# Retention attention and a SoLU layer on one core: chunks paired on halves of the partitions, 64x64 products, u centred

## Chip, cores and metric

One core of one Trainium2 chip. The time is device time in microseconds, from the first to the last instruction of a launch and what lies around them; the median of three runs of the kernel before is 229.86 us (229.05 to 230.84).

## The reference

```python
# q, k, v: [8 batches, 8 heads, 576 tokens, 64]
scores = scale * np.matmul(q, k.transpose(0, 1, 3, 2))        # scale = 1/8
gamma = 1.0 - 2.0 ** (-5.0 - np.arange(H))
Dmat = np.where(rel >= 0, gamma[:, None, None] ** rel, 0.0)   # rel = query - key
x = np.matmul(scores * Dmat, v)          # tokens of all heads side by side: [4608, 512]
h = x @ w_in                             # [4608, 1024]
e = np.exp(h - max(h)); sm = e / (sum(e) + 1e-9)
solu = h * sm
ln = (solu - mean(solu)) / np.sqrt(var(solu) + 1e-6) * g_ln
out = ln @ w_out                         # [4608, 512]
```

The decay is a product of a power for the query, one for the key and a mask, so the attention can run chunk by chunk: within a chunk with scores, across chunks with a state per head (64x64) that is scaled by gamma^128 from chunk to chunk.

## The kernel before

The 4608 tokens are 36 chunks of 128 tokens: four whole chunks of each batch, two batches in turn, and a ninth chunk that holds the last 64 tokens of both. For each chunk n the steps are:

- `lq`, `lk`, `lv`: load 128 tokens x 8 heads x 64 in f32 through the queue of SP (line 150). `q`, `k`, `v`: cast to f16, with the decay powers on q and v (lines 171 to 175, mostly on GpSimd, POOL).
- `tp`: eight transposes of q and k on TensorE (line 200); `qkT`: their copy out of PSUM (line 208).
- `sc`: scores, keys x queries, eight matmuls on a half of the rows each (line 221); `m0`, `m1`: the mask, on VectorE (DVE), 512 columns each (line 229).
- `kp`: the chunk's own contribution to the state, k times v (line 249); `t`: added to the state before (294, 296); `s16`, `s32`: the scaled state, in f16 with zeros beside each head's block, and in f32 (303, 313).
- `xs` (state times q, line 268) and `xv` (masked scores times v, line 282) make x transposed in PSUM; `xT` copies it out.
- `mm1`: h, 8 matmuls of 512 columns (342). `max`, `exp`, `solu` (359, 374, 410): u = h * exp(h - max), with its sum; `nmu`: minus its mean (420); `sq`: the sum of (u - mean)^2 on ScalarE (ACT, 438); `w1`, `w2`, `pow`: the row's scale `rs` (401, 446, 452).
- `lp`: eight transposes of u (460), `uT`: copy out, `mm2`: 8 matmuls of 512 columns (476), `osb`: scaled by `rs` (488, 492), `st`: store (502).

The mean of u is not taken off u: the columns of `w_out` are centred once at the start instead. `ws` scales `w_out` by `g_ln`, `mean` multiplies it by a tile of ones (549), and `cw` subtracts (560).

The order of all steps is written out: `FIRST`, then `LOOP` for chunks 12 to 29, then `LAST`. Every engine, and the queue of SP, takes its instructions in that order. PSUM has four banks in turn for all small products and two pairs of banks for h. `warm` issues matmuls on zeros early on.

Of the kernel before, what the change touches and what calls it, by code (L numbers as in the profile page):

```python
# [17 lines left out]
def _np_tables():  # L18


    g = 1.0 - 2.0 ** (-5.0 - np.arange(H, dtype=np.float64))
    p = np.arange(P)
    gq = (g[None, :] ** p[:, None]) / 8.0
    gk = g[None, :] ** (-p[:, None])
    gqt = (g[None, :] ** (p % 64)[:, None]) / 8.0
    gkt = g[None, :] ** (-(p % 64)[:, None])


    gs = np.zeros((P, 4))
    gd = np.zeros((P, 4, 2))  # L30
    for e in range(2):
        for hp in range(4):
            gs[e * 64 : e * 64 + 64, hp] = g[2 * hp + e] ** 128.0
        gd[e * 64 : e * 64 + 64, :, e] = gs[e * 64 : e * 64 + 64]
    small = np.concatenate([gq, gk, gqt, gkt, gs, gd.reshape(P, 8)], axis=1).astype(np.float32)
    return small
# [3 lines left out]
def kernel(  # L40
# [19 lines left out]
    small_np = _np_tables()  # L60

    const = ctx.enter_context(tc.tile_pool(name="const", bufs=1))
    load = ctx.enter_context(tc.tile_pool(name="load", bufs=8))
    qh = ctx.enter_context(tc.tile_pool(name="qh", bufs=4))
    kvh = ctx.enter_context(tc.tile_pool(name="kvh", bufs=6))
    att = ctx.enter_context(tc.tile_pool(name="att", bufs=3))
    stp = ctx.enter_context(tc.tile_pool(name="stp", bufs=2))
    moe = ctx.enter_context(tc.tile_pool(name="moe", bufs=3))
    two = ctx.enter_context(tc.tile_pool(name="two", bufs=2))
    dead = ctx.enter_context(tc.tile_pool(name="dead", bufs=1))  # L70
    utp = ctx.enter_context(tc.tile_pool(name="utp", bufs=5))
    tiny = ctx.enter_context(tc.tile_pool(name="tiny", bufs=6))
    ps = ctx.enter_context(tc.tile_pool(name="ps", bufs=1, space=bass.MemoryType.PSUM))
    ps_h = ctx.enter_context(tc.tile_pool(name="ps_h", bufs=1, space=bass.MemoryType.PSUM))


    chunks = []
    for g in range(B // 2):
        for c in range(4):
            chunks += [((2 * g,), c), ((2 * g + 1,), c)]  # L80
        chunks.append(((2 * g, 2 * g + 1), 4))
    NCH = len(chunks)

    def rows(n):
        bs, c = chunks[n]
        if c < 4:
            return [(slice(0, P), bs[0], c * P)]
        return [(slice(64 * i, 64 * i + 64), b, 4 * P) for i, b in enumerate(bs)]

    small = const.tile([P, 44], FP, name="small")  # L90
    tris = const.tile([P, 2, P], FP, name="tris")
    ident = const.tile([P, P], F16, name="ident")
    ones = const.tile([P, P], F16, name="ones")
    zeros = const.tile([P, 512], F16, name="zeros")
    mhalf = const.tile([P, 1], FP, name="mhalf")
    gln = const.tile([P, NF], FP, name="gln")
    g32 = const.tile([P, NF], FP, name="g32")
    w_in32 = const.tile([P, 4, DFF], FP, name="w_in32")
    w_out32 = const.tile([P, NF, DM], FP, name="w_out32")
    w_in16 = const.tile([P, 4, DFF], F16, name="w_in16")  # L100
    w_raw16 = const.tile([P, NF, DM], F16, name="w_raw16")
    w_out16 = const.tile([P, NF, DM], F16, name="w_out16")
    mean_sb = const.tile([P, DM], FP, name="mean_sb")
    gq, gk = small[:, 0:8], small[:, 8:16]
    gqt, gkt = small[:, 16:24], small[:, 24:32]
    gs = small[:, 32:36]
    gd = small[:, 36:44].rearrange("p (a b) -> p a b", a=4)

    T = {}

# [9 lines left out]
    def new(key, make):  # L120

        if key not in T:
            T[key] = make()
        return T[key]


    turn = {"bank": 0, "h": 0}

    def bank(shape, dtype, name):
        turn["bank"] += 1  # L130
        return ps.tile(shape, dtype, tag=f"bank{turn['bank'] % 4}", name=name)

    def h_banks(name):
        turn["h"] += 1
        return ps_h.tile([P, DFF], FP, tag=f"h{turn['h'] % 2}", name=name)


# [6 lines left out]


    def load_rows(name, src, n):
        t = load.tile([P, H, D], FP, name=name)
        for pp, b, s0 in rows(n):
            m = pp.stop - pp.start
            nc.sync.dma_start(  # L150
                out=t[pp], in_=src[b, :, s0 : s0 + m, :].rearrange("h p d -> p h d")
            )
        T[name, n] = t

    @step
    def lq(n, j, eng):
        load_rows("qf", q, n)

    @step
    def lk(n, j, eng):  # L160
        load_rows("kf", k, n)

    @step
    def lv(n, j, eng):
        load_rows("vf", v, n)

    def cast(name, to, pool, n, eng, table):
        src = T.get((name, n))
        t = pool.tile([P, H, D], F16, name=to)
        if table is None:  # L170
            copy(eng, t, src)
        else:
            vec(eng).tensor_tensor(  # L173
                out=t, in0=src, in1=table.unsqueeze(2).to_broadcast([P, H, D]), op=ALU.mult
            )
        T[to, n] = t

    def is_tail(n):
        return chunks[n][1] == 4

    @step
    def q_(n, j, eng):
        cast("qf", "q16", qh, n, eng or "g", gqt if is_tail(n) else gq)

    @step
    def k_(n, j, eng):
        cast("kf", "k16", kvh, n, eng or "g", None)

    @step
    def v_(n, j, eng):  # L190
        cast("vf", "v16", kvh, n, eng or "g", gkt if is_tail(n) else gk)


    @step
    def tp(n, j, eng):
        t = bank([P, 2, 4, P], F16, "tp")
        for i, src in enumerate((T.get(("q16", n)), T["k16", n])):
            s2 = src.rearrange("p h d -> p (h d)")
            for hp in range(4):
                nc.tensor.transpose(  # L200
                    out=t[:, i, hp], in_=s2[:, hp * P : (hp + 1) * P], identity=ident
                )
        T["tp", n] = t

    @step
    def qkT(n, j, eng):
        t = att.tile([P, 2, 4, P], F16, name="qkT")
        copy(
            eng or "v", t.rearrange("p a b c -> p (a b c)"),
            T.get(("tp", n)).rearrange("p a b c -> p (a b c)"),  # L210
        )
        T["qkT", n] = t

    @step
    def sc(n, j, eng):
        t = T["qkT", n]
        s = [bank([P, 4, P], FP, f"sc{e}") for e in range(2)]
        for hp in range(4):
            for e in range(2):
                dd = slice(64 * e, 64 * e + 64)  # L220
                nc.tensor.matmul(  # L221
                    out=s[e][:, hp], lhsT=t[dd, 1, hp], rhs=t[dd, 0, hp], start=True, stop=True,
                )
        T["sc", n, 0], T["sc", n, 1] = s

    def mask(n, e):
        i = 1 if is_tail(n) else 0
        r = att.tile([P, 4, P], F16, name=f"ret{e}")
        nc.vector.tensor_tensor(  # L229
            out=r, in0=T.get(("sc", n, e)), in1=tris[:, i : i + 1].to_broadcast([P, 4, P]),  # L230
            op=ALU.mult,
        )
        T["ret", n, e] = r

    @step
    def m0(n, j, eng):
        mask(n, 0)

    @step
    def m1(n, j, eng):  # L240
        mask(n, 1)

    @step
    def kp(n, j, eng):
        t = bank([P, 4, D], FP, "kp")
        k16, v16 = T.get(("k16", n)), T["v16", n]
        for hp in range(4):
            for e in range(2):
                nc.tensor.matmul(  # L249
                    out=t[64 * e : 64 * e + 64, hp], lhsT=k16[:, 2 * hp + e],  # L250
                    rhs=v16[:, 2 * hp + e], start=True, stop=True,
                )
        T["kp", n] = t


    def x_tile(n):
        first = ("x", n) not in T
        return first, new(("x", n), lambda: bank([P, 4, P], FP, "x"))

    @step  # L260
    def xs(n, j, eng):
        bs, c = chunks[n]
        first, x = x_tile(n)
        t = T["qkT", n]
        w = P // len(bs)
        for hp in range(4):
            for i, b in enumerate(bs):
                nc.tensor.matmul(  # L268
                    out=x[:, hp, i * w : (i + 1) * w],
                    lhsT=T["s16", b, c][:, hp].rearrange("p e d -> p (e d)"),  # L270
                    rhs=t[:, 0, hp, i * w : (i + 1) * w],
                    start=first, stop=True, skip_group_check=True,
                )
                first = False

    @step
    def xv(n, j, eng):
        first, x = x_tile(n)
        v16 = T["v16", n]
        for hp in range(4):  # L280
            for e in range(2):
# [420 lines left out]
```

## Time and profile before

| | |
|---|---|
| median of three runs | 229.86 us |
| span of the profiled execution, first to last instruction (its own time beside it is not listed) | 228.4 us |
| busy: PE, DVE, ACT, POOL | 216.1, 190.8, 167.1, 169.4 us |
| mean granted TensorE clock | 0.991 |
| moved by DMA | 42.34 MB in 120795 packets, 114496 of them under 512 B |

All figures of the trace come from one execution. PE is TensorE's matmuls, PEld its weight loads, SPq what the queue of SP issues. Lnnn is a line of the kernel that the profile belongs to. In the timeline a row is: start, length, engine, line, operation, tiles, how many were merged. A matmul's length has its way through the array in it, so the pace of a row of matmuls is read from the starts. Groups have: busy time, mean length in ns, and the idle time before them with what ended it.

### The profile page before, as it was taken

What the parts mean: (1) busy time and instruction counts of PE and PEld (TensorE: products, weight loads), DVE (VectorE), ACT (ScalarE), POOL (GpSimd) and SP (SyncE); (2) the same over time, 40 slices, a digit from 0 to 9 for tenths busy, and PEclk for the clock granted to TensorE, in tenths of its full rate; (3) what the DMA queues carried; (4) which work ended last, traced back from release to release, by engine and by line L of the source; (5) the groups of instructions that cost most, each with busy time, mean ns of one, the idle gap of its engine ahead of it and who ended that gap; (6) DMA issues with size and microseconds to landing.
All of it is one profiled execution on the core that took longest, in us unless ns stands there. A gap on an engine that the chain in (4) does not pass through costs nothing.

```text
span 228.4 us, 5672 instructions
## 1 busy us (share of the span) xinstructions
PE 216.1 (95%) x2181; PEld 122.1 (53%) x2181; DVE 190.8 (84%) x346; ACT 167.1 (73%) x270; POOL 169.4 (74%) x244
## 2 busy tenths in 40 slices
PE   7879689899999999999999999999999999999991
PEld 2334255555655655556555555555665565555461
DVE  1229999999997995899989999999889999898740
ACT  2075459877879799777778777777898777849970
POOL 2234999789969969799858998999958998655320
PEclk9999889999999999999999999999999999999999
DMA  6999999999999599999999887898955064111125
GB/s 159 250 353 312 231 228 206 212 197 191 244 225 239 110 236 236 254 221 265 216 264 218 188 198 156 204 226 180 211 144 138 3 176 103 47 49 47 46 74 159
DMA packets 120795, 42.34 MB, mean 185 GB/s; under 512 B 114496, under 2 KB 114752, under 8 KB 120768
## 3 DMA queue, kind: packets, MB, share of 16 engines
q1 hardware_dynamic: 119728, 41.98, 80.9%
q8 instruction: 17, 0.28, 0.6%
q10 hardware_dynamic: 1040, 0.00, 0.2%
q14 instruction: 10, 0.08, 0.1%
HBM read 32.53 MB, written 9.44 MB: 184 GB/s over the span
## 4 chain that ended last, share of the span: by engine, by line
PE 81%; DVE 8%; SPq 4%; DMA 3%; issue 1%; ACT 1%; DVEq 0%; ACTq 0%
PE o L476 27%; PE h L342 26%; PE lp L460 7%; PE tp L200 6%; PE sc L221 4%; PE x L282 4%; DMA vf<-in_v_dram 3%; PE x L268 3%; PE kp L249 3%; SPq L150 2%; DVE w_out L560 2%; DVE nm L359 1%; SPq L522 1%; DVE ret L229 1%; PE hh L332 1%
## 5 line engine op out<-in xcount | busy, mean ns | idle before, releaser
L342 PE MATMUL h<-w_in,xT 128*128 128x512 f16 x280 | 67.8, 387 | 1.6 <-DVE xT L118 1.5
L476 PE MATMUL o<-w_out,uT 128*128 128x512 f16 (+1 forms) x296 | 67.6, 373 | 0.0
L303 POOL TENSOR_TENSOR s<-t,small 128x512 f16<-128x512 f32 x32 | 33.5, 1048 | 19.7 <-DVE t L296 10.7
L229 DVE TENSOR_TENSOR ret<-sc,tris 128x512 f16<-128x512 f32 x72 | 46.4, 679 | 1.1 <-PE sc L221 1.0
L410 DVE SCALAR_TENSOR_TENSOR u<-h,e 128x1024 f16<-128x1024 f32 x35 | 42.6, 1217 | 2.6 <-ACT e L374 2.6
L173 POOL TENSOR_TENSOR q<-qf,small 128x512 f16<-128x512 f32 x35 | 36.9, 1055 | 9.8 <-DMA qf<-in_q_dram 9.8
L359 DVE TENSOR_REDUCE nm<-h 128x1 f32<-128x1024 f32 x35 | 42.5, 1214 | 1.4 <-PE h L342 1.3
L374 ACT ACTIVATE e<-h,nm 128x1024 f32<-128x1024 f32 x35 | 38.9, 1111 | 6.4 <-DVE nm L359 6.3
L438 ACT ACTIVATE sq<-u,nmu 128x1024 f16<-128x1024 f16 (+1 forms) x37 | 41.7, 1129 | 0.1
L476 PEld LDWEIGHTS <-uT 128*128 128x128 f16 x296 | 27.3, 98 | 26.9
L342 PEld LDWEIGHTS <-xT 128*128 128x128 f16 x280 | 26.1, 99 | 28.9 <-issue 2.3
L116 ACT CAST xT<-x 128x512 f16<-128x512 f32 x34 | 19.9, 584 | 25.8 <-PE x L268 19.3
L173 POOL TENSOR_TENSOR v<-vf,small 128x512 f16<-128x512 f32 x34 | 35.8, 1055 | 0.0
L116 ACT COPY uT<-lp 128x1024 f16<-128x1024 f16 x33 | 33.3, 1013 | 2.5 <-PE lp L460 2.5
L452 POOL TENSOR_TENSOR rs<-w,mhalf 128x1 f32<-128x1 f32 x36 | 20.1, 560 | 13.8 <-DVE w L446 11.9
L492 ACT ACTIVATE o_sb<-o,rs 128x512 f32<-128x512 f32 (+1 forms) x36 | 24.5, 681 | 5.7 <-PE o L476 3.1
L118 DVE COPY qkT<-tp 128x1024 f16<-128x1024 f16 x30 | 20.6, 686 | 6.2 <-PE tp L200 5.8
L460 PE MATMUL lp<-ident,u 128*128 128x128 f16 x288 | 21.7, 219 | 0.8 <-DVE u L410 0.6
L118 POOL CAST k<-kf 128x512 f16<-128x512 f32 x31 | 19.3, 624 | 1.8 <-PE lp L460 1.8
L460 PEld LDWEIGHTS <-u 128*128 128x128 f16 x288 | 17.6, 98 | 2.9 <-DVE u L410 0.7
L221 PE MATMUL sc<-qkT 64*128 64x128 f16 x288 | 14.3, 218 | 2.8 <-DVE t L294 1.5
L313 POOL TENSOR_TENSOR s<-t,small 128x256 f32<-128x256 f32 x24 | 15.1, 630 | 1.6 <-DVE w L446 1.0
(63 smaller groups left out, 241.5 us busy)
## 6 DMA issues: line engine op xcount, KB each, us to landing
qf<-in_q_dram SPq DMA_DIRECT2D x32, 256.0 KB, 4.4
kf<-in_k_dram SPq DMA_DIRECT2D x32, 256.0 KB, 5.1
vf<-in_v_dram SPq DMA_DIRECT2D x32, 256.0 KB, 4.8
out_dram<-o_sb SPq DMA_DIRECT2D x32, 256.0 KB, 2.7
w_out<-in_moe_w_out_dram SPq DMA_DIRECT2D x4, 512.0 KB, 5.4
w_in<-in_moe_w_in_dram SPq DMA_DIRECT2D x4, 512.0 KB, 6.5
qf<-in_q_dram SPq DMA_DIRECT2D x8, 128.0 KB, 3.6
kf<-in_k_dram SPq DMA_DIRECT2D x8, 128.0 KB, 4.9
```

The costliest lines, as they stand in the source:

```text
L116: nc.scalar.copy(out=out, in_=in_)
L118: vec(eng).tensor_copy(out=out, in_=in_)
L173: vec(eng).tensor_tensor(out=t, in0=src, in1=table.unsqueeze(2).to_broadcast([P, H, D]), op=ALU.mult)
L229: nc.vector.tensor_tensor(out=r, in0=T.get(("sc", n, e)), in1=tris[:, i : i + 1].to_broadcast([P, 4, P]), op=ALU.mult,)
L303: nc.gpsimd.tensor_tensor(out=s, in0=T["t", n].unsqueeze(2).to_broadcast([P, 4, 2, D]), in1=gd.unsqueeze(3).to_broadcast([P, 4, 2, D]), op ...
L342: nc.tensor.matmul(out=h[:, i * 512 : (i + 1) * 512], lhsT=s[:, d], rhs=w_in16[:, d, i * 512 : (i + 1) * 512], start=r == 1, stop=r == 4,)
L359: nc.vector.tensor_reduce(out=nm, in_=T[key("h", n, j)], axis=AX.X, op=ALU.max, negate=True)
L374: nc.scalar.activation(out=e, in_=T[key("h", n, j)], func=ACT.Exp, bias=T["nm", n], accum_out=s)
L410: nc.vector.scalar_tensor_tensor(out=u, in0=T.get(key("h", n, j)), scalar=1.0, in1=T.get(key("e", n, j)), op0=ALU.mult, op1=ALU.mult, accu ...
L438: nc.scalar.activation(out=t, in_=T[key("u", n, j)], func=ACT.Square, bias=T["nmu", n], accum_out=ss)
L460: nc.tensor.transpose(out=t[:, c], in_=u[:, c * P : (c + 1) * P], identity=ident)
L476: nc.tensor.matmul(out=o, lhsT=T["uT", n][:, c], rhs=wt[:, c, a : a + w], start=c == 0, stop=c == NF - 1,)
```

## The change

Nearly all of the kernel is written anew; the computation is the same but for where the mean of u is taken off. What differs:

- A pair n is now the same 128 tokens of two batches. Batch x lies on partitions 64x to 64x + 63, and the two halves of 64 tokens lie side by side in the free dimension. There are 16 pairs of 2 x 128 tokens and four short ones of 2 x 64. Each load is 64 tokens of one batch, 128 KB; a cast of k covers a whole pair. Loads go through a ring of 14 slots; the early weights pass through the same ring.
- `sc`, `kp`, `xs` and `xv` are products of 64 rows by 64 columns of the array, so that four, on four quarters, could run at the same time. Of the 2x2 blocks of 64 keys by 64 queries the upper one (later keys, earlier queries) is not computed; a mask covers 2 x 2 x 192 columns.
- In pairs from 2 on, batch 1 has the two heads of each couple in swapped halves of x transposed (`crossed`), and `mm1` then takes `w_x16`, a copy of `w_in16` with its halves of rows swapped, made by two DMAs (`wx`).
- `fx`: VectorE reads eight elements of the x banks between `xs` and `xv`.
- `uc`: u plus minus its mean, in f16, on VectorE. `lp` and `sq` read it. `mean` and `cw` of `w_out` are gone; `cw` now names the cast of `w_in`.
- Copies of f16 tiles from PSUM by ScalarE (`qT`, `kT`, `uT`) are made as half as many f32 words.
- All eight PSUM banks are one tensor; the plan names the banks of each step behind a slash. One plan, `PLAN`, gives the order of everything.

```diff
+    pairs = [(g, c) for g in range(B // 2) for c in range(5)]
+    def crossed(n):
+        return CROSS and n >= CROSS and not short(n)          # CROSS = 2
...
+    def load(name, src, n, j):
+        for s in halves(n, j):
+            for x in range(2):
+                r = 64 * (2 * c + s)
+                nc.sync.dma_start(
+                    out=t[64 * x : 64 * x + 64, s],
+                    in_=src[2 * g + x, :, r : r + 64, :].rearrange("h p d -> p h d"),
+                )
...
+    def back(name, n, j, eng):
+        if eng == "s":
+            copy("s", words(t)[:, w], pb[:, b, w])
...
     def sc(n, j, eng, bs):
-                nc.tensor.matmul(
-                    out=s[e][:, hp], lhsT=t[dd, 1, hp], rhs=t[dd, 0, hp], start=True, stop=True,
-                )
+        def one(e, hp, key, a, b):
+            r = slice(64 * e, 64 * e + 64)
+            o = scores(n, j, bs, e, hp)[:, 64 * (a - lo) : 64 * (b - lo)]
+            for x in range(2):
+                c = slice(64 * x, 64 * x + 64)
+                nc.tensor.matmul(
+                    out=o[c], lhsT=kt[r, key, hp, c],
+                    rhs=qt[r, a - key : b - key, hp, c], start=True, stop=True,
+                )
...
+    def xs(n, j, eng, bs):
+        def one(x, e, hp):
+            r = slice(64 * e, 64 * e + 64)
+            o = pb[:, bs[x]].rearrange("p (a c) -> p a c", a=4)
+            nc.tensor.matmul(
+                out=o[out_half(n, x, e), hp, a:b], lhsT=st[r, x, hp],
+                rhs=qt[r, hs, hp, 64 * x : 64 * x + 64],
+                start=hp == 0, stop=True, skip_group_check=True,
+            )
...
+    def fx(n, j, eng, bs):
+        nc.vector.tensor_copy(
+            out=buf("fence", 0, 1, [P, 2, 4], FP), in_=banks(T["x", n, j])[:, :, 0:512:128]
+        )
...
     def kp(n, j, eng, bs):
+            for e in range(2):
+                nc.tensor.matmul(
+                    out=o[64 * e : 64 * e + 64, hp], lhsT=k16[r, s, 2 * hp + e],
+                    rhs=v16[r, s, 2 * hp + e], start=s == 0 and hp == 0, stop=True,
...
     def mm1(m, j, eng, bs):
+        s, w = xt(m), weights(m)               # w_x16 for the second tile of a crossed pair
...
     def uc(m, j, eng, bs):
+        nc.vector.tensor_scalar(
+            out=uc_of(m)[:, cols(j)], in0=u_of(m)[:, cols(j)], scalar1=tiny("nmu", m),
+            scalar2=None, op0=ALU.add, op1=ALU.bypass,
+        )
     def sq(m, j, eng, bs):
-            out=t, in_=T[key("u", n, j)], func=ACT.Square, bias=T["nmu", n], accum_out=ss
+            out=buf("sq", 0, 1, [P, DFF], F16)[:, cols(j)], in_=uc_of(m)[:, cols(j)],
+            func=ACT.Square, accum_out=tiny("ss", m, j),
...
     def uT(m, j, eng, bs):
+        if (eng or "s") == "s":
+            copy("s", words(t)[:, a : a + w], pb[:, b, 0:w])
...
+    def wx(n, j, eng, bs):
+        for y in range(2):
+            nc.sync.dma_start(
+                out=w_x16[64 * y : 64 * y + 64], in_=w_in16[64 * (1 - y) : 64 * (1 - y) + 64]
+            )
-    def mean(n, j, eng):
...
+    PLAN = """
+        lk:0.0 lq:0.0 q:0.0@v lq:0.1 q:0.1@v k:0.0@s warm:16/7 tk:0.0/0 kT:0.0@s lk:0.1 k:0.1@v
+        lv:0.0 warm:4/2 tq:0.0/1 qT:0.0@s warm:2/4 sc:0.0/23 tq:0.1/4 qT:0.1@s lv:0.1 m0:0.0
+        warm:2/6 tk:0.1/5 wi:0 kT:0.1@s cw:0.1@s wi:1 cw:1.0@s v:0.0@v warm:2/0 sc:0.1/67 m0:0.1
...
+        xs:3/01 fx:3 exp:4 osb:2@s solu:4 nmu:4 uc:4 v:3@g kp:3/45 t:3 xv:3 xT:6@s wx xT:7@s
+        mm1:5/23 max:5 lk:4 sq:4 mm1:6/67 w1:4 k:4@g w2:4 lk:5 max:6 exp:5 s16:3@g lp:4/0 mm1:7/45
...
```

More of the change, by code (lines that the diff above doesn't have):

```diff
@@ L143, in step, with halves, span @@
         return f
[L146 to L151, printed above, removed]
-            )
-        T[name, n] = t
+    def halves(n, j):
+        if j is not None:
+            return [j]
+        return [0] if short(n) else [0, 1]
+    def span(n, j):
+        hs = halves(n, j)
+        return slice(hs[0], hs[-1] + 1)
```

835 lines of the change are left out of this document (456 added, 379 removed).

## The prediction

> **What bounds the kernel now.** I read the totals of the page first, then the busy time by stretches, then one period of TensorE in order of time.
>
> ```profile
> PE 216.1 (95%) x2181; PEld 122.1 (53%) x2181; DVE 190.8 (84%) x346; ACT 167.1 (73%) x270; POOL 169.4 (74%) x244
> PE 81%; DVE 8%; SPq 4%; DMA 3%; issue 1%; ACT 1%; DVEq 0%; ACTq 0%
> ```
> ```profile
> 0.00:45.00 45.00, 37.51 (x316) 19.06 (x317) 31.67 (x49) 24.45 (x35) 27.37 (x39) 0.96 1.08 245
> 45.00:85.00 40.00, 39.87 (x433) 22.88 (x432) 37.96 (x73) 32.28 (x54) 35.31 (x50) 1.00 0.98 205
> 85.00:195.00 110.00, 110.00 (x1179) 63.90 (x1177) 98.65 (x177) 87.83 (x143) 93.58 (x135) 1.00 0.84 188
> 195.00:228.40 33.40, 28.70 (x262) 16.28 (x260) 22.56 (x50) 22.55 (x41) 13.11 (x23) 0.99 0.21 72
> ```
>
> The second fence gives, for each stretch, its length and the busy time of PE, PEld, DVE, ACT and POOL, then clock, DMA share and GB/s. From 45 us on TensorE never rests, and the chain is TensorE's. But VectorE is close behind: it is busy 98.65 of 110 us. It idles 13.3 us of the first 45, 2.0 + 11.4 = 13.4 us between 45 and 195, and 10.8 us at the end. An edit that frees TensorE gains only as far as VectorE can follow.
>
> ```profile
> 117.27 1.89 PE L342 MATMUL h<-w_in,xT 128*128 128x512 f16 x8
> 119.09 0.32 PE L249 MATMUL kp<-v,k 128*64 128x64 f16 x8
> 119.24 0.39 PE L282 MATMUL x<-ret,v 128*64 128x128 f16 x8
> 119.56 0.40 PE L221 MATMUL sc<-qkT 64*128 64x128 f16 x8
> 119.93 1.89 PE L476 MATMUL o<-w_out,uT 128*128 128x512 f16 x8
> 121.65 0.39 PE L200 MATMUL tp<-ident,q 128*128 128x128 f16 x4
> 122.10 0.61 PE L460 MATMUL lp<-ident,u 128*128 128x128 f16 x8
> 122.54 1.89 PE L342 MATMUL h<-w_in,xT 128*128 128x512 f16 x8
> ```
>
> The lengths contain each matmul's tail, so the cost is the distance between starts. `lp`: 8 transposes in 0.44 us, 0.055 us for 128 columns. `mm2` takes 1.72 us, 0.215 for 512 columns; `mm1` takes 1.82, so about 0.09 more stands between it and `kp`, which uses another shape of the array (128x64 instead of 128x128). `xv`: 8 matmuls of 128 columns in 0.32 us, less than the 0.44 that they would take in a row. If two on different column halves run together they need 4 x 0.055 = 0.22, and 0.10 is again the change of shape before `sc`. `sc`, on row halves, takes 0.37: 0.22 and a longer change. `kp`, 8 of 64 columns, takes 0.15; four pairs of 0.028 are 0.11. So pairs run side by side on column halves and on row halves, and a change of shape costs about 0.093.
>
> **TensorE, part by part.** After the change `sc`, `kp`, `xs` and `xv` are 64x64 products, four quarters of the array. I take four at a time, as the product of the two pairings shown; bounds are four at a time and two at a time. Counts are from the instruction order of both kernels.
>
> - Before, two at a time: `kp` 256/2 x 0.028 = 3.6; `sc` and `xv` each 288/2 x 0.055 = 7.9; `xs` one at a time, 96 x 0.055 + 32 x 0.028 = 6.2. Together 25.6 us.
> - After, four at a time: `sc` and `xv` each have 240 of 128 columns and 352 of 64 (the upper block is left out), 60 x 0.055 + 88 x 0.028 = 5.8; `kp` 512/4 x 0.028 = 3.6; `xs` 176 crossed at 0.055/4, 16 at 0.055/2, 64 at 0.028/2 = 3.8. Together 19.0. Gain 6.6 us; at two at a time all of it costs about 36, a loss of 10.
> - Changes of shape: 127 before, 90 after, 37 x 0.093 = 3.4 us gained.
>
> The number of these products doubles (960 to 1952). The Trainium skill, "TensorEngine Tiling (Array Packing)", section "Gotcha 2: Feature Incompatibilities", excludes Fast Weight Load under column tiling, and "TensorE: Matmul & The Clock Gate", section "LDWEIGHTS", gives columns/1.2 ns, 53 ns for 64 columns. By it each of the 336 sets of four with 64 columns would take 53 and not 28 ns, an estimate of 8.4 us more. The `kp` row disagrees: four pairs at 53 ns are 0.21 us, and it took 0.15.
>
> **The start.** In order of time the chain has:
>
> ```profile
> 10.10 7.92 DMA vf<-in_v_dram
> 25.77 5.31 PE h L342 x16
> 33.91 1.83 PE h L342 x8
> 37.83 1.90 PE h L342 x8
> 45.48 1.73 PE o L476 x8
> 48.70 1.40 PE h L342 x6
> ```
>
> By 47 us the kernel has done four `mm1` and one `mm2`. The `v` that ends the first wait is queued behind all of `w_out` and a quarter of `w_in`, because the column means of `w_out` are wanted early. The change centres u instead, so `w_in` (2.1 MB) goes right after the first pair (1.6 MB): 3.7 MB at the 0.245 MB/us of the first window is 15 us, and the first `mm1` can start near 17. Then come pair 1 (1.6), `w_out` (2.1), pairs 2 and 3 (3.1) and the crossed copy of `w_in` (1.0): 11.5 MB, 47 us, for tile 5's `mm1`, which needs that copy. In front of it stand five `mm1` and four `mm2`, four blocks more than before: 6.9 us. DVE and POOL must convert in step with these loads, so I take 5, with bounds 0 and 9. The 8 matmuls of the mean (1.7 us) lie inside the start.
>
> TensorE alone: 228.4 - 6.6 - 3.4 - 5 = 213.4 us.
>
> **VectorE, part by part.**
>
> ```profile
> L229 DVE TENSOR_TENSOR ret<-sc,tris 128x512 f16<-128x512 f32 x72 | 46.4, 679 | 1.1 <-PE sc L221 1.0
> L359 DVE TENSOR_REDUCE nm<-h 128x1 f32<-128x1024 f32 x35 | 42.5, 1214 | 1.4 <-PE h L342 1.3
> L118 DVE COPY qkT<-tp 128x1024 f16<-128x1024 f16 x30 | 20.6, 686 | 6.2 <-PE tp L200 5.8
> L446 DVE TENSOR_TENSOR w<-w,ss 128x1 f32<-128x1 f32 x36 | 10.3, 292 | 1.4 <-ACT sq L438 0.8 <-POOL w L401 0.5
> L296 DVE TENSOR_TENSOR t<-kp,s 128x256 f32<-128x256 f32 x24 | 9.8, 417 | 0.8 <-PE kp L249 0.7
> L560 DVE SCALAR_TENSOR_TENSOR w_out<-w_out,g,mean_sb 128x512 f16<-128x512 f32 x8 | 9.3, 1188 | 0.0
> L420 DVE TENSOR_SCALAR nmu<-su 128x1 f32<-128x1 f32 x36 | 5.2, 149 | 0.8
> L173 DVE TENSOR_TENSOR v<-vf,small 128x512 f16<-128x512 f32 x2 | 1.4, 692 | 0.7 <-DMA vf<-in_v_dram 0.7
> L488 DVE TENSOR_SCALAR o_sb<-o,rs 128x256 f32<-128x256 f32 x1 | 0.5, 483 | 2.1 <-PE o L476 2.1
> ```
> ```profile
> 15.43 1.09 DVE L536 TENSOR_SCALAR w_raw<-w_out,g 128x512 f16<-128x512 f32 x1 [4.61 <-DMA w_out<-in_moe_w_out_dram]
> 17.37 0.47 DVE L536 TENSOR_SCALAR w_raw<-w_out,g 128x512 f16<-128x512 f32 x1
> 15.19 1.04 POOL L541 TENSOR_TENSOR w_raw<-w_out,g 128x512 f16<-128x512 f32 x1
> 97.07 0.61 POOL L118 CAST k<-kf 128x512 f16<-128x512 f32 x1
> 97.25 0.45 DVE L446 TENSOR_TENSOR w<-w,ss 128x1 f32<-128x1 f32 x1
> 113.68 0.15 DVE L446 TENSOR_TENSOR w<-w,ss 128x1 f32<-128x1 f32 x1
> ```
>
> From 512 to 1024 f32 the price rises by 1.214 - 0.679 = 0.535, about 1.045 ns an element.
>
> - Masks: 72 x 0.679 = 48.9 become 30 of 768 elements (0.946), one of 1024 and five of 512: 33.0. -15.9.
> - Copies of turned f16 tiles: most go to ACT; 22 fewer at 0.686, two more halves at 0.42, as the 256 f32 of `t`: -14.3.
> - Centring of `w_out`: -8 x 1.188 = -9.5. State `t`: 16 at 0.685 (0.417 and 256 more elements) for 32 at 0.417: -2.5.
> - `osb`: nine tiles at 0.483 + 0.267 = 0.75 and a half more: +7.2. `xT`: six more, priced as the masks of 512: +4.1. Casts: four q or v at 0.692, three of `w_in` at 0.47: +4.2.
> - `fx`: 16 reads of eight elements, at most the 0.149 of the smallest row: +2.4.
> - `uc`: no row has this f16 operation. `w_raw` at 17.37 converts 512 f32 in 0.47, where a cast with two inputs takes 0.69; and the `qkT` copy moves 1024 f16 in the time in which a mask handles 512 f32. Both together make 1024 f16 cost what 512 f32 cost, 0.47; if only one holds it is 0.74. I take 0.47: +17.1 (26.6 at the other end).
>
> Sum -7.2: 183.6 us. To this comes a wait. The same `w_raw` took 1.09 us when a POOL operation had begun before it: 15.43 + 1.09 is 0.29 after POOL's end at 16.23, so it began its work only then. `w2` took 0.45 while POOL cast k and ended with it, and 0.15 with POOL idle. `uc` is of this kind. The mean wait of `w2` was 0.292 - 0.15 = 0.14; that of this `w_raw` was 1.09 - 0.47 = 0.62. `uc` comes right behind `nmu`, as `w2` does at 97.25, so I take 0.25, nearer the first: 35 waits are 8.8 us (bounds 4.9 and 21.7): VectorE 192.4.
>
> With some 10.5 us of idle at a shorter start and the 10.8 of the end that is 213.7 us, the same as TensorE. Two engines equally full, each waiting for the other through `sc`, masks and `xv`, do not both run without gaps. The gaps of VectorE in the middle were 13.4 us; I take 5, bounds 0 and 13.4. `fx` adds a wait: VectorE stops in order until `xs` is through, with `max`, masks and `solu` queued behind it, and `xv` waits for it. Mostly `kp` or an `mm` block stands between `xs` and `xv`, which covers it; without that cover it is some 0.3 us each, 5 us, within those bounds.
>
> 213.7 + 5 = 218.7 us of span; the median of the runs before lies 229.86 - 228.4 = 1.5 above the span: **220 us**.
>
> **What is not on the path.**
>
> ```profile
> L116 ACT COPY uT<-lp 128x1024 f16<-128x1024 f16 x33 | 33.3, 1013 | 2.5 <-PE lp L460 2.5
> L116 ACT CAST xT<-x 128x512 f16<-128x512 f32 x34 | 19.9, 584 | 25.8 <-PE x L268 19.3
> L303 POOL TENSOR_TENSOR s<-t,small 128x512 f16<-128x512 f32 x32 | 33.5, 1048 | 19.7 <-DVE t L296 10.7
> ```
> ```profile
> 123.50 0.43 SPq L150 DMA_DIRECT2D qf<-in_q_dram  x1
> 128.77 1.31 SPq L150 DMA_DIRECT2D qf<-in_q_dram  x2
> ```
>
> As 512 words `uT` costs what `xT` costs: 30 x 0.43 = 13 us less on ACT, and the q and k copies put about that back; `osb` and `xT` leave 10. ACT stays near 155. POOL loses 16 of the s16 steps, 17 us, and stays under 150. SP issues 216 loads of 64 rows instead of 120, at about 0.43 to 0.65 each: 93 to 140 us of a 220 us span, so there is room, but every store stands in the same queue in front of later loads.
>
> **Rivals.**
>
> 1. The lock costs little and the order fits: TensorE alone sets the end, 213.4 + 1.5 = 215, down to 211 with the full 9 us at the start. For it: TensorE ran without a gap from 85 to 195. Chance 0.25.
> 2. VectorE becomes the bound with its old gaps: 213.7 + 13.4 = 227.1, 228.6 as a time: no change. For it: 98.65 of 110 us already. Against: those gaps were waits for a TensorE that was the bound. Chance 0.12.
> 3. Slower: the 64x64 products run two at a time. TensorE is 17 us longer than forecast: 213.4 + 17 + 1.5 = 232, with 2 us of gaps 234. It decides as soon as a set of four takes over twice 0.028 or 0.055. Against it: both pairings are in the rows. Chance 0.13.
> 4. The change does not do what it says for the weights: narrow loads of weights set the pace of `kp` and the short blocks. By the bound from rows, `kp` at 0.15/4 = 0.038 a set and not 0.028, 336 sets cost 3.4 more, 223 in all. Chance 0.05. The estimate of 8.4 from the two pages above would make it 228.
>
> **How the numbers follow.** The forecast, both engines full, 214 to 226, has 0.45 and gives 220. The range goes to 209 below and to 232 above, where half of the third rival lies outside. Faster by over 1% (the least that this kernel's measurement can tell from no change): forecast, 1, 4 and a little of 2, 0.76. Within 1%: most of 2, 0.10. Slower: 3 and the worst waits, 0.14.
>
> **What would show it.** Right: `sc` of 32 matmuls starts to the next group 0.33 us later (0.43 with a change of shape), `kp` of 32 in 0.22; the first `h` before 18 us and four `o` blocks by 47; `uc` near 0.47 at best and 0.7 in the mean; DVE busy about 192 us, over 95% between 85 and 195; the chain shared by PE and DVE. Wrong: `sc` at 0.66 or `kp` at 0.44 (rival 3); `uc` at 0.74 with POOL idle; TensorE resting over 10% in the middle, or waits on loads there.

## The result, and the profile after

The changed kernel takes **251.44 us** (median of four runs, 250.6 to 252.6) against 229.87: 1.093 times the time before, 95% interval 1.087 to 1.099. The forecast was 220, the range 209 to 232. Times are medians of all executions of a kernel; ratios leave out executions more than 1.5% above its fastest.

The profiled execution has a span of 249.0 us. First its totals and the shares of the chain that ended last, by engine and by line:

```profile
PE 215.7 (87%) x3175; PEld 120.8 (49%) x3175; DVE 196.3 (79%) x342; ACT 152.9 (61%) x278; POOL 146.0 (59%) x196
SPq 28%; PE 26%; DVE 16%; DMA 15%; issue 5%; POOL 5%; ACT 3%; DVEq 0%; ACTq 0%; POOLq 0%
```

The chain was 81% TensorE's before. Now its largest part is SPq, the queue on which SP issues transfers; with DMA it is 43%. The busy time by stretches (length, then PE, PEld, DVE, ACT, POOL, clock, DMA share, GB/s):

```profile
0.00:45.00 45.00, 38.47 (x481) 19.62 (x482) 27.02 (x46) 21.56 (x38) 22.16 (x36) 1.00 0.88 211
45.00:85.00 40.00, 34.26 (x516) 19.03 (x515) 34.04 (x55) 23.25 (x43) 24.91 (x30) 0.96 0.81 192
85.00:195.00 110.00, 94.63 (x1524) 55.23 (x1522) 89.08 (x155) 72.00 (x129) 74.98 (x96) 0.97 0.79 193
195.00:249.00 54.00, 48.35 (x659) 26.93 (x657) 46.13 (x89) 36.13 (x69) 23.97 (x37) 0.99 0.32 94
```

Between 85 and 195 us TensorE is busy 94.6 of 110 us, where it had no gap before, and VectorE 89.1, less than before. Neither is full: both wait. For what, the waits of POOL say (total, times, longest):

```profile
POOL k L117 <- DMA ring<-in_k_dram: 16.3, 8, 4.3
POOL v L191 <- DMA ring<-in_v_dram: 15.1, 6, 9.7
POOL q L191 <- DMA ring<-in_q_dram: 12.3, 11, 2.6
```

44 us of waits for loaded data, on the engine that converts it; before, such waits were 9.8 us, all for q. (The granted clock is no rival for the 21 us lost: it is 0.5 for 3.4 us at 57 us and for 6.8 us at 125 us, which lengthens the steps between matmuls of 512 columns by 2.9 us in all, against 1.8 in the kernel before.) The queue in order of time, first before, then after:

```profile
118.67 0.43 SPq L150 DMA_DIRECT2D qf<-in_q_dram  x1
119.21 0.65 SPq L150 DMA_DIRECT2D kf<-in_k_dram  x1
119.90 0.81 SPq L150 DMA_DIRECT2D vf<-in_v_dram  x1
123.10 0.36 SPq L502 DMA_DIRECT2D out_dram<-o_sb  x1
```
```profile
99.68 0.63 SPq L165 DMA_DIRECT2D ring<-in_q_dram  x1
100.36 6.67 SPq L165 DMA_DIRECT2D ring<-in_v_dram  x8
107.07 2.67 SPq L165 DMA_DIRECT2D ring<-in_k_dram  x4
109.84 0.57 SPq L657 DMA_DIRECT2D out_dram<-osb  x1
110.51 1.16 SPq L654 DMA_DIRECT2D out_dram<-osb  x2
```

Before, three issues of 128 tokens, 256 KB each, feed a tile, and then the queue rests until the next `o_sb` is ready (120.71 to 123.10). After, 12 issues of 64 tokens and 128 KB feed a pair, and they stand back to back, four in 2.67 us. Over all 216 the median issue is 0.633 us (least 0.595) and the next begins 0.045 later: 146 us for the loads alone. The rests of the queue, before and after (total, times, longest):

```profile
SPq L502 <- ACT o_sb L492: 73.4, 23, 9.5
```
```profile
SPq L657 <- ACT osb L643: 24.6, 6, 8.6
```

Of the 73.4 us, 13.7 lie between 85 and 150 us; of the 24.6, none do, and 21.6 come behind 187 us, when few loads are left. From 85 to 150 us SP starts 88 transfers, whose issues fill 59.5 us; the small gaps make up the other 5.5. In the kernel before 59 fill 46.3 us. **The queue is full, and it is the pace of the kernel.** An issue of half the bytes takes one and a half times the 0.43 us that the first of the three takes after a rest.

### The profile page after: what moved, and what is told of

It is laid out like the page before. It is cut to its first block, busy times and chain, and to the rows that moved or that the text cites. A ratio compares the mean times of both kernels' runs of the same rounds, so it can differ in the third digit from the quotient of the medians.

```text
span 249.0 us, 7816 instructions
## 1 busy us (share of the span) xinstructions
PE 215.7 (87%) x3175; PEld 120.8 (49%) x3175; DVE 196.3 (79%) x342; ACT 152.9 (61%) x278; POOL 146.0 (59%) x196
## 4 chain that ended last, share of the span: by engine, by line
SPq 28%; PE 26%; DVE 16%; DMA 15%; issue 5%; POOL 5%; ACT 3%; DVEq 0%; ACTq 0%; POOLq 0%
SPq L165 23%; PE pb L623 10%; PE pb L483 7%; DMA ring<-in_q_dram 5%; DMA ring<-in_v_dram 4%; DVE u L558 4%; DVE nm L501 3%; DMA ring<-in_k_dram 3%; DMA ring<-in_moe_w_out_dram 3%; DVE ret L303 3%; PE pb L601 3%; POOL v L191 2%; DVE uc L572 2%; SPq L654 2%; PE pb L391 1%
## 5 line engine op out<-in xcount | busy, mean ns | idle before, releaser
L623 PE MATMUL pb<-w_out,uT 128*128 128x512 f16 (+1 forms) x296 | 67.0, 374 | 5.6 <-DVE uT L117 2.5
L526 ACT ACTIVATE e<-pb,nm 128x1024 f32<-128x1024 f32 (+1 forms) x37 | 40.4, 1092 | 17.9 <-DVE nm L501 15.0
L501 DVE TENSOR_REDUCE nm<-pb 128x1 f32<-128x1024 f32 x35 | 42.3, 1217 | 10.2 <-PE pb L483 10.0
L191 POOL TENSOR_TENSOR v<-ring,small 128x512 f16<-128x512 f32 x35 | 36.9, 1072 | 15.1 <-DMA ring<-in_v_dram 15.1
L558 DVE SCALAR_TENSOR_TENSOR u<-pb,e 128x1024 f16<-128x1024 f32 (+1 forms) x37 | 43.9, 1187 | 0.6 <-ACT e L526 0.2
L579 ACT ACTIVATE sq<-uc 128x1024 f16<-128x1024 f16 (+1 forms) x37 | 38.4, 1039 | 9.0 <-DVE uc L572 7.1
L483 PE MATMUL pb<-w_in,xT 128*128 128x512 f16 x168 | 39.9, 379 | 1.9 <-DVE w_in L117 1.7
L191 POOL TENSOR_TENSOR q<-ring,small 128x512 f16<-128x512 f32 x30 | 31.5, 1060 | 14.8 <-DMA ring<-in_q_dram 12.3
L303 DVE TENSOR_TENSOR ret<-pb,keep 128x768 f16<-128x768 f32 (+2 forms) x36 | 32.0, 917 | 0.5 <-PE pb L279 0.5
L483 PE MATMUL pb<-w_x,xT 128*128 128x512 f16 x112 | 29.5, 411 | 2.6 <-DMA w_x<-w_in 2.6
L572 DVE TENSOR_SCALAR uc<-u,nmu 128x1024 f16<-128x1024 f16 (+1 forms) x37 | 26.5, 719 | 1.0
L601 PE MATMUL pb<-ident,uc 128*128 128x128 f16 x288 | 21.6, 220 | 2.9 <-DVE uc L572 2.9
```

The costliest lines, as they stand in the source:

```text
L191: vec(eng).tensor_tensor(out=t, in0=src, in1=table[:, s].unsqueeze(2).to_broadcast([P, H, D]), op=ALU.mult,)
L303: nc.vector.tensor_tensor(out=ret(n)[:, :, k * i : k * i + k, 64 * lo : 64 * hi], in0=banks(bs)[:, :, 0 : k * w].rearrange("p e (a c) -> p ...
L483: nc.tensor.matmul(out=pb[:, bs[i]], lhsT=s[:, d], rhs=w[:, d, i * 512 : (i + 1) * 512], start=r == 1, stop=r == 4,)
L501: nc.vector.tensor_reduce(out=tiny("nm", m, j), in_=h_of(m, j), axis=AX.X if j is not None else AX.XY, op=ALU.max, negate=True,)
L526: nc.scalar.activation(out=like_h(e_of(m), j), in_=h_of(m, j), func=ACT.Exp, bias=tiny("nm", m), accum_out=tiny("s", m, j),)
L558: nc.vector.scalar_tensor_tensor(out=like_h(u_of(m), j), in0=h_of(m, j), scalar=1.0, in1=like_h(e_of(m), j), op0=ALU.mult, op1=ALU.mult, a ...
```

## Experiments

**1. Whole issues again.** The long pairs from 1 on are loaded as two issues of 128 tokens in place of four of 64. The tokens then lie on other partitions, so the output is not the reference's; every operation of the compute engines and its size stay.

```diff
     def load(name, src, n, j):
+        if j is None and not short(n):
+            for s in range(2):
+                nc.sync.dma_start(out=t[:, s],
+                    in_=src[2 * g + s, :, P * c : P * c + P, :].rearrange("h p d -> p h d"))
+            return
```

> The changed kernel, but each long pair after the first is loaded as before the change: one issue of 128 tokens of one batch (256 KB) in place of two of 64 tokens, 126 loads in place of 216, the same bytes and packets. The tokens land on other partitions than the products assume, so the output is not the reference's; the instructions are the same. Theory A (the queue of SP is the bound: 216 issues at 0.63 us and 0.045 between them keep it busy to about 190 us): 90 issues fewer, 114 at 0.68 become 114 x 0.5, some 65 us less work for SP; time falls to 218 to 226 us, POOL's waits for loads (44 us) fall below 15. Theory B (the order of steps and the coupling of VectorE and TensorE set the time, loads are late only because their slots come free late): 245 us or more.

230.71 us, 1.003 times the time before (1.000 to 1.006). So the form of the load issues is worth 20.7 us, nearly all of the loss. The chain and the stretch from 85 to 195 us:

```profile
PE 43%; DVE 30%; SPq 10%; issue 5%; POOL 5%; DMA 3%; ACT 2%; DVEq 0%; POOLq 0%; ACTq 0%
85.00:195.00 110.00, 103.79 (x1709) 60.61 (x1707) 104.03 (x176) 82.10 (x149) 79.51 (x101) 1.00 0.85 196
```

The chain belongs to TensorE and VectorE, as forecast, and POOL's waits for q, k and v fall from 44 to 18 us, 15 of them in the first 45. But the time lies 5 us above the 218 to 226 expected: the change gains nothing with whole issues either, and something else of the forecast's sum is missing. Nor is the queue idle now: between 85 and 150 us 63 issues fill 60.9 us, since a load issue takes 0.94 us in the median there, while the DMA engines' busy share is 1.01 (next experiment).

**2. The same price in the kernel before.** Each load of 128 tokens there becomes two of 64, nothing else.

```diff
-            nc.sync.dma_start(
-                out=t[pp], in_=src[b, :, s0 : s0 + m, :].rearrange("h p d -> p h d"))
+            for i in range(0, m, 64):
+                nc.sync.dma_start(out=t[pp.start + i : pp.start + i + 64],
+                    in_=src[b, :, s0 + i : s0 + i + 64, :].rearrange("h p d -> p h d"))
```

> The kernel before with each load of 128 tokens split into two issues of 64 tokens, 216 loads instead of 120, everything else as it was. Theory A: SP's loads take 147 us instead of about 60 to 110, and it also waited 73 us for osb; the loads lose their lead: 234 to 245 us. Theory B: 229 to 232 us, as the kernel before.

239.9 us, 1.042 (1.038 to 1.047). The queue, then DMA in the stretch from 85 to 150 us (length, clock, DMA share, GB/s) in four kernels: before, this one, after, and the first experiment:

```profile
99.40 1.36 SPq L151 DMA_DIRECT2D qf<-in_q_dram  x2
100.86 1.27 SPq L151 DMA_DIRECT2D kf<-in_k_dram  x2
102.18 1.31 SPq L151 DMA_DIRECT2D vf<-in_v_dram  x2
```
```profile
85.00:150.00 65.00, 1.00 1.00 221
```
```profile
85.00:150.00 65.00, 1.00 0.82 202
```
```profile
85.00:150.00 65.00, 0.95 0.81 195
```
```profile
85.00:150.00 65.00, 1.00 1.01 230
```

With whole issues the 16 DMA engines are full in this stretch (the share of the view can come out above 1); with halves they fall to 0.82, because the queue gives them no more: it is issuing for 57.6 of the 65 us. The kernel before has nothing of the rest of the change, and the halves alone cost it 10 us. The Trainium skill, "DMA: Bandwidth & Descriptors", section "Rules for kernel authors", advises one transfer over 128 partitions in place of two to the halves. The trace agrees with the advice. The reason given there, that both share the same DMA engines, is not what cost the time here: those had time to spare, and the issuing queue had almost none.

**3. Bytes or partitions?** The loads of the kernel before are cut by heads: 128 KB each as after, but over all 128 partitions.

```diff
-            nc.sync.dma_start(
-                out=t[pp], in_=src[b, :, s0 : s0 + m, :].rearrange("h p d -> p h d"))
+            for i in range(0, H, 4):
+                nc.sync.dma_start(out=t[pp, i : i + 4],
+                    in_=src[b, i : i + 4, s0 : s0 + m, :].rearrange("h p d -> p h d"))
```

> The kernel before with each load split in two by heads: 240 issues of 128 KB, but each still over 128 partitions (tails over 64). As many issues and bytes per issue as in e3, which took 0.633 us each over 64 partitions. If the price goes by the partitions: 0.40 to 0.45 us for most, 228 to 233 us. If it goes by bytes or by packets: 0.6 us or more, 237 to 242 us.

234.5 us, 1.017 (1.011 to 1.023), between the two forecasts.

```profile
65.36 1.00 SPq L151 DMA_DIRECT2D qf<-in_q_dram  x2
66.41 1.17 SPq L151 DMA_DIRECT2D kf<-in_k_dram  x2
67.63 1.08 SPq L151 DMA_DIRECT2D vf<-in_v_dram  x2
```

Two issues with the gap between them take 1.00 to 1.17 us, some 0.5 each (0.51 in the median of all), where two of the same bytes on 64 partitions took 1.27 to 1.36. So the number of issues costs, and the half partitions cost on top of it. What in the queue makes 64 partitions dearer stays open.

**4. The stores out of the way.** Is the queue late because loads stand behind stores that wait for their tile? Only the words `st` of the step order move, each behind the next four load steps, with eight tiles `osb` in place of four.

```diff
-        mm1:8/67 solu:7 nmu:7 uc:7 st:0 osb:4@v qT:5@s
+        mm1:8/67 solu:7 nmu:7 uc:7 osb:4@v qT:5@s
...
+        tq:6/5 sq:8 exp:9 w2:7 qT:6@v lq:7 st:0 w1:8 q:7@g
...
-        return buf("osb", m, 4, [P, DM], FP)[:, a : a + w], w, a
+        return buf("osb", m, 8, [P, DM], FP)[:, a : a + w], w, a
```

> The kernel after, every store put four load steps later in SP's order and eight output tiles in place of four; the other engines' orders are the same. Theory A1, the queue is late because its loads stand behind stores that wait for their tile (39 us of waits for osb): without these waits its 216 loads of 0.633 and its stores, 147 + 24 us, fit under the span, and the time falls to 231 to 240. Theory A2, the rate of the issues alone keeps the loads late, with or without the waits: 245 to 252.

251.34 us, 1.088 (1.078 to 1.097): nothing gained, as A2 says. The rate of the issues is the limit, not what stands between them. The kept trace is of an execution of 256.2 us at a mean granted clock of 0.84, so its stages can't be compared with after's. In it 162 loads are started by 150 us, 159 after.

**5. Stores, or q, on ScalarE's queue.** All stores on ACT's queue, and, in another kernel, the q loads from pair 2 on.

```diff
-        q_ = nc.scalar if eng == "s" else nc.sync
+        q_ = nc.scalar
```
```diff
-                nc.sync.dma_start(
+                (nc.scalar if name == "q" and n > 1 else nc.sync).dma_start(
```

> The changed kernel with all stores issued from ACT's queue and none from SP's. Theory A: SP loses 44 issues (24 us) and the 39 us in which a store waited at its head for osb; loads alone are 216 x 0.68 = 147 us, with the weights and the full queue of the start about 175: 230 to 238 us. Theory B: ACT gets 20 us of issues, VectorE and TensorE keep their order: 248 to 254 us.

> The changed kernel with the loads of q of pairs 2 to 19 issued from ACT's queue, 64 of the 216; the output is the reference's. Theory A: SP loses 44 us of issues, ACT (153 us busy of 249) gets them, and stalls there where a slot of the ring is not yet free: 225 to 238 us. Theory B: 249 to 260 us, from ACT's stalls.

266.40 us (1.145, 1.141 to 1.148) and 280.33 (1.217, 1.210 to 1.224): both worse than after, and above the ranges of both theories. The waits of SP with the stores moved (in an execution of 269.2 us), and of POOL with q moved:

```profile
SPq L165 <- DMA out_dram<-osb: 41.6, 12, 7.4
```
```profile
POOL q L191 <- DMA ring<-in_q_dram: 42.3, 18, 5.0
```

With the stores on the other queue, waits of SP's loads are put down to the landing of stores; in the kernel after none are. The trace only infers what ended a wait, and what ties the two together was not separated. With q on ScalarE's queue, q comes late. Its issues stand in order among ScalarE's own work, which would explain it; no run shows that alone. In these two kernels the second queue cost more than it freed.

**6. A version that computes the reference.** q is read only through its transposes, so its tokens may lie in any order: the long pairs from 1 on load q in whole issues, and `sc` and `xs` read the turned q by batch. k and v cannot, since they meet on the same half of the partitions.

```diff
+        if name == "q" and by_rows(n):
+            for x in range(2):
+                nc.sync.dma_start(out=t[:, x],
+                    in_=src[2 * g + x, :, P * c : P * c + P, :].rearrange("h p d -> p h d"))
+            return
...
-                    rhs=qt[r, a - key : b - key, hp, c], start=True, stop=True,
+                    rhs=qt[r, x, hp, 64 * (a - key) : 64 * (b - key)] if by_rows(n)
+                    else qt[r, a - key : b - key, hp, c], start=True, stop=True,
```

> The kernel after, with q of the long pairs from 1 on loaded as two issues of 128 tokens (q is only read through its transposes, so its tokens may lie in any order; the q table has a column set for that order). SP issues 186 loads in place of 216: 30 issues of about 0.47 us for 60 of 0.68, 26 us less queue time. Theory A, the queue's rate sets the time: SP then needs 6.4 us of loads for a pair, under the 9.3 that a pair took before, the last load starts 18 to 26 us earlier than at 209 us, and the time falls to 230 to 237. Theory F, it is the landing of the 64-token loads (k and v) and not the queue's total that keeps the engines waiting: 242 to 250.

242.30 us, 1.058 (1.049 to 1.067): 9.1 us less than after, where 18 to 26 of queue time were to come free. The first experiment replaced 180 half issues and gained 20.7 us; this one replaces 60 of them, a third, and gains 44% of that. Theory A had the direction and not the size: the 30 whole issues took 0.63 us in the median and not 0.47, so less queue time came free: all load issues together take 150.0 us, 160.5 after (and 134.9 in the first experiment). The number lies at the edge of F, but the last load starts 9.0 us earlier and the kernel ends 9.1 earlier, which speaks for the queue. Counted from the traces, loads started, in units of 64 tokens, the start of the last one, and the span of the same execution:

| kernel | by 45 us | by 85 us | by 150 us | last load starts | span |
|---|---|---|---|---|---|
| before | 54 | 108 | 186 | 186.9 | 228.4 |
| 1, whole issues | 49 | 98 | 184 | 187.6 | 230.3 |
| 6, q whole | 45 | 89 | 170 | 199.8 | 239.6 |
| after | 43 | 82 | 159 | 208.8 | 249.0 |

In all four the span ends 39.8 to 42.7 us behind the start of the last load, with the work that is left then. In the kernel before the queue rests for its consumers; after, they wait for the queue. That is the simplest reading of the result: **the last load starts 22 us later, and the span is 20.6 us longer.** The table alone does not show which causes which; the first two experiments do. And the start of the last load does not set the end in every kernel: in the trace of experiment 4 it comes at 196.6 us, 57.9 before the end, and with `uc` on ScalarE (experiment 7) 47.5 before it.

**7. VectorE.** With the first experiment's loads, `uc` is left out (`lp` and `sq` read u uncentred, so the output is not the reference's); then `uc` is put on ScalarE.

```diff
     def uc(m, j, eng, bs):
-        nc.vector.tensor_scalar(...)
+        return
```
```diff
-        nc.vector.tensor_scalar(...)
+        nc.scalar.activation(out=uc_of(m)[:, cols(j)], in_=u_of(m)[:, cols(j)],
+            func=ACT.Identity, bias=tiny("nmu", m))
```

> The kernel of e1 (128-token loads, output not the reference's) with the centring of u on VectorE left out as well: lp and sq read u. Theory C (once the loads come in time VectorE is the bound, with uc's 26 us, a third of them waits for POOL): VectorE falls from 200 to about 174 us and TensorE, 209 busy with its gaps, is left as the bound: 212 to 221 us. Theory D (the start and the order of steps keep the time): 226 us or more.

> The kernel of e1 with uc on ScalarE instead of VectorE, at the same place of the order. Theory C: VectorE falls to about 174 us, ACT rises from 153 to about 192, no more waits of uc for POOL; ACT's longer chain gives part of it back: 214 to 224 us. Theory D: 228 us or more.

Without `uc`: 228.94 us, 0.991 (0.987 to 0.995). On ScalarE: 250.51, 1.086 (1.078 to 1.093). The stretch from 85 to 195 us without it, and `uc` in the first experiment and on ScalarE:

```profile
85.00:195.00 110.00, 103.57 (x1717) 60.70 (x1706) 91.15 (x156) 82.27 (x149) 78.28 (x103) 1.00 0.87 200
```
```profile
L579 DVE TENSOR_SCALAR uc<-u,nmu 128x1024 f16<-128x1024 f16 (+1 forms) x37 | 28.4, 769 | 1.0
```
```profile
L579 ACT ACTIVATE uc<-u,nmu 128x1024 f16<-128x1024 f16 (+1 forms) x37 | 41.5, 1129 | 10.2 <-DVE nmu L572 10.0
```

VectorE falls from 104.0 to 91.2 us, and TensorE's busy time stays where it was (103.8 and 103.6). So VectorE is not the bound of the first experiment, although it looked full. The opposite move costs 20 us: 1.13 us on ScalarE for the 0.77 that `uc` took on VectorE, in the middle of each tile's path. The order of the steps is fixed; in these two runs a shorter step gained little in it and a longer one lost much. Theory D names both times, 226 and 228 us or more, though not the size of the second; which wait of that kernel costs the 20 us was not taken apart.

**8. The start.** In the kernel before, `w_in` goes ahead of `w_out`, and the column means come after the second `mm1`.

```diff
-        lq:0 q:0@v wo:2 lq:1 lk:0 lv:1 lk:1 wo:1 k:1@s wo:3 q:1@g wo:0 g32 ws:6@g warm:32 tp:1
+        lq:0 q:0@v lq:1 lk:0 lv:1 lk:1 lv:0 wi:2 k:1@s wi:0 q:1@g wi:1 wi:3 k:0@g warm:32 tp:1
```

> The kernel before with another order up to its third mm1: v of chunk 0 and w_in are loaded ahead of w_out, and the mean of w_out is made after the first two mm1; everything is computed. If the start is limited by what stands in SP's queue, the first mm1 comes near 17 us instead of 25.8 and TensorE, the bound from then on, ends earlier: 222 to 227 us. If the bytes of the first 45 us are the limit whatever their order: 229 to 233 us.

234.81 us, 1.020 (1.014 to 1.026), slower than both forecasts. The products of `w_in` in that kernel:

```profile
17.64 3.63 PE L342 MATMUL h<-w_in,xT 128*128 128x512 f16 x16
28.39 3.17 PE L549 MATMUL mean<-w_raw,ones 128*128 128x512 f16 x8
35.36 0.82 PE L342 MATMUL h<-w_in,xT 128*128 128x512 f16 x3
```

The first two tiles' `mm1` come 8 us earlier, as meant, and the third at 35.36 in place of 33.84. What is drawn forward seems to be paid back by what it overtakes; the rest of the loss was not taken apart. Two further kernels put it to the changed kernel: the first experiment with pair 0 too in whole issues (six for twelve; the output is not the reference's), and the sixth with pair 0's k issued by ScalarE.

```diff
-        if j is None and not short(n):
-            for s in range(2):
+        if not short(n):
+            for s in halves(n, j):
```
```diff
-                nc.sync.dma_start(
+                (nc.scalar if name == "k" and n == 0 else nc.sync).dma_start(
...
-        lk:0.0 lq:0.0 q:0.0@v lq:0.1 q:0.1@v k:0.0@s warm:16/7 tk:0.0/0 kT:0.0@s lk:0.1 k:0.1@v
+        lk:0.0 lq:0.0 lk:0.1 q:0.0@v lq:0.1 q:0.1@v k:0.0@s warm:16/7 tk:0.0/0 kT:0.0@s k:0.1@v
```

> The kernel of the run with 128-token loads, with pair 0 loaded in whole issues of 128 tokens too (6 issues in place of 12; tokens again land on other partitions, so the output is not the reference's). Theory S, SP's issues hold the start: its first twelve issues (0.8 to 9.0 us) become six of 0.43, some 5 us earlier for w_in and all that follows, and the time goes from 230.7 to 225 to 228. Theory T, the start is held by the transfers themselves (DMA share 0.97 over the first 45 us) and by the chain behind them, not by the issues: 229.5 to 231.5.

> The same with the four k loads of pair 0 issued from ScalarE's queue, which has nothing else to do in the first 6 us: SP reaches w_in after 8 issues (6.2 us) in place of 12 (9.0). Theory S, SP's issues hold the start: 2 to 3 us less than the run with q alone changed. Theory T, the transfers hold it: within 1 us of that run.

The first gave 227.2 to 231.2 us, median 229.5 (228.2 in the profiled execution, span 226.1); before, on the same chip, 229.97. The second 241.66, ratio 1.047 (1.039 to 1.056), within 1 us of 242.30: T. The first settles nothing: its median stands at the edge of T, its profiled execution between S and T.

No version that computes the reference beat the kernel before.

## Why the prediction was wrong

**The step that failed** stands under "What is not on the path": SP issues 216 loads "at about 0.43 to 0.65 each: 93 to 140 us of a 220 us span, so there is room". The price of half loads was there in the row of two q loads in 1.31 us, the upper end, and at the median of 0.633 with its gap the loads do cost 146 us; their lengths as measured sum to 160.5. Wrong was "so there is room". The queue also issues 44 stores (24 us) and the weights; in the first 45 us it gets only 43 loads out, many at 1.1 to 1.4 us each; and the budget was not 220 us but the 187 by which the last load started before. In a sum that followed TensorE and VectorE alone the queue had no place, and no rival was built on it: the chance of 0.14 for a slower kernel stood on other reasons. What the runs showed in its place: the load issues are worth 20.7 of the 21.6 us lost against the kernel before (experiment 1), and in that kernel the halves alone cost 10 (experiment 2).

The other steps, against TensorE's account, counted from the starts of the matmuls in the traces and good to some 2 us. Its useful time counts every matmul at the least distance to the next of its kind, 0.216 us for 512 columns and 0.056 for 128, and warm-up products at nothing; the rest is lost. Useful in all: 185.2 us before, 178.2 after. Lost up to:

| | 45 us | 85 us | 195 us |
|---|---|---|---|
| before | 26.5 | 30.5 | 36.7 |
| after | 26.3 | 36.5 | 61.6 |
| 1, whole issues | 25.4 | 31.1 | 43.9 |
| 8, pair 0 too | 22.1 | 29.3 | 42.1 |

- *Products four at a time, -6.6 us: held, somewhat smaller.* In the useful time these products have 27.1 us before and 21.9 after, 5.2 less; the mean's 1.7 make up the 7.0. One period of TensorE:

```profile
160.64 0.42 PE L334 MATMUL pb<-qT,s 64*64 64x128 f16 x16
160.93 0.45 PE L367 MATMUL pb<-v,k 64*64 64x64 f16 x32
165.74 0.54 PE L279 MATMUL pb<-qT,kT 64*64 64x128 f16 x32
166.22 0.62 PE L215 MATMUL pb<-ident,q 128*128 128x128 f16 x8
```

  `sc` of 32 starts to the next group 0.48 us later, 0.43 with the change of shape forecast; two at a time would be 0.66 and more. From first to last start `kp` of 32 takes 0.254 us in the median, 31 products in fours: 0.033 for a set. Rival 3 falls, and of rival 4 about half of its 3.4 us is left. At the 0.053 of the Trainium skill, "TensorE: Matmul & The Clock Gate", section "LDWEIGHTS", for each set, the 0.254 would be 0.41, an estimate; the trace disagrees.
- *Changes of shape, -3.4: held.* A step from one shape to another costs 0.095 us over the least distance, in the median of both kernels; that is 12.1 us for the 127 before and 8.6 for the 90 after. It counts as lost time in the table.
- *The start, -5: failed.* The first `mm1` comes at 14.35 us, earlier than forecast, but by 47 us TensorE has done four `mm1` and three `mm2`, seven for the nine forecast, and lost as much as before. (The kernel before had done five `mm1` by then and not four, so nine would have been three blocks more, 5.2 us, and not 6.9.)

```profile
14.35 0.59 PE L483 MATMUL pb<-w_in,xT 128*128 128x512 f16 x2
```
```profile
9.05 2.04 SPq L668 DMA_DIRECT2D ring<-in_moe_w_in_dram  x4
15.65 5.71 SPq L165 DMA_DIRECT2D ring<-in_k_dram  x4
26.20 1.60 SPq L684 DMA_DIRECT2D ring<-in_moe_w_out_dram  x3
```

  Twelve half issues put `w_in` at 9.05 us, and those of pair 1, 1.1 us each in the mean, put `w_out` at 25 to 28. The forecast counted megabytes only. With all of pair 0 in whole issues too, 4.4 us of the 5 are there. That the issues gave them is not shown: without `uc` (experiment 7), with pair 0 still in halves, TensorE is busy 40.57 of the first 45 us, against 41.65 here and 38.34 in the first experiment.
- *VectorE 183.6 and a wait of 8.8, 192.4 us: held*, 196.3. The price of `uc`, taken as 0.47 from rows far off, and its wait, together forecast as 0.72 in the mean, are in these rows, as is that of `fx`:

```profile
L572 DVE TENSOR_SCALAR uc<-u,nmu 128x1024 f16<-128x1024 f16 (+1 forms) x37 | 26.5, 719 | 1.0
L355 DVE COPY fence<-pb 128x8 f32<-128x8 f32 x16 | 2.5, 159 | 8.8 <-PE pb L334 4.9 <-issue 3.8
177.44 0.49 DVE L572 TENSOR_SCALAR uc<-u,nmu 128x1024 f16<-128x1024 f16 x1
170.54 1.28 DVE L572 TENSOR_SCALAR uc<-u,nmu 128x1024 f16<-128x1024 f16 x1
```

  That VectorE sets the end with TensorE was wrong all the same (experiment 7).
- *The lock-step gaps, +5: too small.* They are the second error, hidden behind the queue. With pair 0 too in whole issues TensorE loses 7.2 us between 45 and 85 us and 12.8 from there to 195, before 4.0 and 6.2: 9.8 more. Waits over 0.15 us between 85 and 195 us sum to 0.6 us in 4 places before and to 8.0 in 18 there, the longest 2.2, where `xs` waits for POOL's `s16`. The whole then reads: 228.4 - 4.4 (start) - 7.0 (useful) + 9.8 = 226.8, against a span of 226.1. Being an account, it must come out so; it shows where the time went and not why. That two full engines wait for each other is only one reading. Most of the loss lies before 113 us, and pieces of that kernel's chain there are:

```profile
45.63 7.08 DMA ring<-in_k_dram
53.51 6.13 DMA ring<-in_q_dram
```
```profile
100.38 5.18 DMA ring<-in_q_dram
105.71 2.70 POOL q L198 x2
108.41 1.01 POOL s L430
109.46 0.44 PE pb L341 x16
```

  The longest wait, that of `xs` at 109.46, ends a chain that begins with a load: POOL casts q and then makes `s16`. The DMA engines' share there is 1.04 between 45 and 85 us and 1.01 from 85 to 113, so the rival is that the transfers themselves, and no longer the queue, hold the loads back. In the kernel before they are as full (0.98 and 1.12) and TensorE has no gap. Whether an order of steps made for these products, or loads with more lead, would close the gaps was not tried.

For the kernel after, the same sum: 228.4 - 0.2 - 7.0 + 6.2 (45 to 85) + 18.9 (85 to 195) + 2.7 behind it is its 249.0.

## What to carry to other kernels

Give the issuing queue a line of its own in the sum, like an engine: the number of its issues by the price of their form, with stores and weights, against the time by which the last load must start, not against the span. A change of layout that halves the partitions of a load doubles its issues, and here an issue of half the bytes cost more than a whole one after a rest. When one limit is lifted, look for the next close behind it: with whole issues the DMA engines, VectorE and TensorE were all above 0.9 between 85 and 150 us, and the gain of the faster products did not arrive. An engine that is 95% busy is not yet the bound; leaving out a piece of its work is the test, and here it gave 0.8%.

## What the runs showed of the hardware

An issue of 128 KB to 64 partitions held SP's queue for 0.63 us in the median (least 0.595), one of 128 KB to 128 partitions for about 0.5, and one of 256 KB to 128 partitions for 0.43 right after a rest of the queue. Among other issues the last was dearer: 0.63 in the median among half loads (experiment 6), and 0.94 between 85 and 150 us of the first experiment, where the DMA engines' share was 1.01. Stores are alike: 64 rows 0.58 (1.16 for two), 128 rows 0.36 after a rest in the kernel before, but 0.57 right behind half loads in the kernel after. Sets of four 64x64 products of 64 columns, on four quarters of the array, followed each other every 0.033 us.
